# Masks of the first three units moved from VectorE to ScalarE and GpSimd, and the first two value tiles loaded from GpSimd's queue

## The chip, the cores and the metric

One core of one Trainium2 chip. The metric is the device time of one execution in microseconds (us); smaller is better. "Before" and "after" are the kernel without and with the change. A kernel is called faster or slower when the interval of its ratio lies beyond 2%.

## The reference

Gated linear attention (4 batches x 8 heads, 768 steps, 48 wide), then a low-rank mixer and an MLP on the result (4 x 768 x 384):

```python
f = 1.0 / (1.0 + np.exp(-f_logit))
for t in range(S):
    state = f[:, :, t, :, None] * state + np.einsum('bhd,bhe->bhde', k[:, :, t], v[:, :, t])
    y[:, :, t] = np.einsum('bhd,bhde->bhe', q[:, :, t], state)
x = y.transpose(0, 2, 1, 3).reshape(B, S, H * D)
xt = x.transpose(0, 2, 1)
u = x + (xt @ U @ V).transpose(0, 2, 1)
return u + np.maximum(u @ w_ch1, 0.0) @ w_ch2
```

## The kernel before

Attention runs in 16 units, each two heads of a batch; `HP` is 4 units per batch. Units 0 to 3 stand alone at the start: there is no MLP work yet to put beside them. Within a unit the sequence is cut into 12 chunks of 64. The parts that matter:

```python
def load(n, *names):                       # f, k, q, v of unit n, all from SyncE's queue
    ...
    nc.sync.dma_start(out=dst[:, :, par, 0:D], in_=head.rearrange("(c p) d -> p c d", p=P))
    ...
load(0, "f", "k", "q")
load(1, "f")
load(0, "v")
load(1, "k", "q", "v")
# ... constants, then eight small GpSimd memsets, then the weight loads are defined

def scores():                              # in attend(n)
    T["A"] = two.tile([P, 2, NBL, C], F32, name="A")
    sc = ps_big.tile([P, 2, 512], F32, name="sc", tag="big")
    # 48 products k^T q into sc (PSUM)
    with tc.high_priority(offset=AHEAD):
        nc.vector.tensor_tensor(T["A"], sc[...], causal..., ALU.mult)     # the mask

def inner():                               # later: 48 products of A with v
    ...

# the first batch, in a fixed order on TensorE, VectorE and ScalarE
busy(1)                                    # dummy products, to keep TensorE going
for piece in front(0, "gates"):
    piece()
for n in range(HP):
    pieces = front(n, "keep", "keys") + rear(n - 1, "scan", "scores")
    pieces += [lambda: busy(3)] + rear(n, "kept") + front(n, "read_back", "queries")
    if n + 1 < HP:
        pieces += front(n + 1, "gates") + rear(n - 1, "read", "inner") + rear(n, "states")
    for piece in pieces:
        piece()
    if n < 2:
        load(n + 2, "v")
    if n == 1:
        for start, _ in weights[: early + 2]:      # the first of these loads U
            start()
    elif n > 1:
        load(n + 2, "f", "k", "q", "v")
```

`gates` turns f on TensorE (six transposes) and takes the sigmoid; once f of unit n is read, f of unit n + 2 is loaded into its place. **One thing matters later**: in this stretch only TensorE, VectorE and ScalarE run in the order written.

## Time and profile before

| | before |
|---|---|
| time, median of the first 3 runs (range) | 488.54 us (488.51 to 489.53) |
| span of the profiled run | 486.9 us |
| TensorE busy | 469.2 us, 96% |
| masks on VectorE | 16 |

Beside the lines that the prediction shows, two more of the page are needed. The first is the clock granted to TensorE in 40 equal slices of the span, in tenths of full speed; the second is the group of VectorE's scans called Y below.

```profile
PEclk9999999999999999999999999999999999999999
L712 DVE TENSOR_TENSOR_SCAN late<-fz,other 128x768 f32<-128x768 f32 x16 | 27.9, 1745 | 0.1
```

Every slice has a 9 (90% or more). The row says less than it seems to: the trace's first clock record, of full speed, begins at 10.99 us, and a stretch without a record is drawn as full speed. Before that TensorE was slower, as the prediction's lines show: six transposes take 1.51 us at 6.60 and 0.85 us at 20.02, the filler 3.43 us and later 2.13. From 10.99 to 485 us the clock did not fall in this run. The scans take 1745 ns each.

### The profile page before, as it was taken

What the parts mean: (1) busy time and instruction counts of PE and PEld (TensorE: products, weight loads), DVE (VectorE), ACT (ScalarE), POOL (GpSimd) and SP (SyncE); (2) the same over time, 40 slices, a digit from 0 to 9 for tenths busy, and PEclk for the clock granted to TensorE, in tenths of its full rate; (3) what the DMA queues carried; (4) which work ended last, traced back from release to release, by engine and by line L of the source; (5) the groups of instructions that cost most, each with busy time, mean ns of one, the idle gap of its engine ahead of it and who ended that gap; (6) DMA issues with size and microseconds to landing.
All of it is one profiled execution on the core that took longest, in us unless ns stands there. A gap on an engine that the chain in (4) does not pass through costs nothing.

```text
span 486.9 us, 12734 instructions
## 1 busy us (share of the span) xinstructions
PE 469.2 (96%) x5541; PEld 400.0 (82%) x5541; DVE 355.4 (73%) x563; ACT 163.2 (34%) x309; POOL 37.6 (8%) x49
## 2 busy tenths in 40 slices
PE   7996899999999999999999999999999999999995
PEld 4775688886566568899898888899979999999995
DVE  5887689777999857656857548797896886958642
ACT  2444666664334313423231403433231312112200
POOL 3002245453000000000000000000000000000000
PEclk9999999999999999999999999999999999999999
DMA  9979975756778512333535100100000000000001
GB/s 146 158 153 178 254 194 135 162 143 79 110 116 121 96 41 36 52 48 67 76 55 94 25 18 18 27 3 20 19 1 1 33 2 18 16 1 34 1 33 38
DMA packets 158679, 34.34 MB, mean 71 GB/s; under 512 B 149206, under 2 KB 157078, under 8 KB 158614
## 3 DMA queue, kind: packets, MB, share of 16 engines
q1 hardware_dynamic: 158614, 33.44, 37.0%
q8 instruction: 45, 0.74, 0.6%
q14 instruction: 20, 0.16, 0.1%
HBM read 28.70 MB, written 4.72 MB: 69 GB/s over the span
## 4 chain that ended last, share of the span: by engine, by line
PE 79%; DVE 10%; DMA 3%; issue 3%; ACT 2%; SPq 2%; DVEq 0%; ACTq 0%
PE pw L312 26%; PE pz L258 23%; PE pp L410 11%; PE y L863 2%; PE pt L660 2%; PE sc L788 2%; PE ds L825 2%; PE y L881 2%; PE po L283 2%; PE idle L962 2%; PE put L246 1%; DMA late<-in_f_logit_dram 1%; DVE late L694 1%; DVE late L712 1%; PE pt L809 1%
## 5 line engine op out<-in xcount | busy, mean ns | idle before, releaser
L258 PE MATMUL pz<-uT,w 128*128 128x256 f32 x504 | 115.7, 383 | 0.3 <-ACT uT L247 0.3
L258 PEld LDWEIGHTS pz<-uT,w 128*128 128x128 f32 x504 | 93.4, 190 | 13.3 <-issue 0.5
L312 PE MATMUL pw<-w,z_all 128*128 128x192 f32 x216 | 37.7, 329 | 0.0
L312 PE MATMUL pw<-zw,w_raw 128*128 128x192 f32 x216 | 37.4, 327 | 0.0
L312 PEld LDWEIGHTS pw<-zw,w_raw 128*128 128x128 f32 x216 | 35.2, 190 | 0.8 <-issue 0.6
L312 PEld LDWEIGHTS pw<-w,z_all 128*128 128x128 f32 x216 | 35.0, 190 | 0.7
L95 POOL TENSOR_TENSOR w<-w_y,w_r 128x384 int32<-128x384 int32 x24 | 31.5, 1311 | 41.5 <-DVE w_y L94 36.5
L694 DVE TENSOR_TENSOR_SCAN late<-fz,late 128x768 f32<-128x768 f32 x16 | 28.1, 1755 | 8.9 <-ACT fz L689 4.2
L268 ACT ACTIVATE z_all<-pz 128x512 f32<-128x512 f32 x33 | 19.7, 596 | 41.4 <-PE pz L258 41.3
L410 PE MATMUL pp<-v_nat,late 128*128 128x128 f32 x224 | 28.8, 275 | 0.0
L712 DVE TENSOR_TENSOR_SCAN late<-fz,other 128x768 f32<-128x768 f32 x16 | 27.9, 1745 | 0.1
L410 PEld LDWEIGHTS pp<-v_nat,late 128*128 128x128 f32 x224 | 27.0, 192 | 0.0
L283 PE MATMUL po<-w,zw 128*128 128x384 f32 x72 | 25.6, 499 | 0.0
L283 PE MATMUL po<-w,z_all 128*128 128x384 f32 x72 | 25.3, 496 | 0.3 <-DVE o L187 0.3
L403 ACT ACTIVATE other<-other 128x512 f32<-128x512 f32 x18 | 11.3, 631 | 39.9 <-DVE other L187 39.9
L851 ACT COPY st<-added 128x576 f32<-128x576 f32 x12 | 14.7, 1224 | 27.5 <-DVE added L846 27.5
L92 DVE TENSOR_SCALAR w_y<-w_y 128x384 f32<-128x384 f32 (+3 forms) x27 | 13.1, 485 | 14.0 <-ACT w_y L90 13.8
L795 DVE TENSOR_TENSOR A<-sc,causal 128x768 f32<-128x768 f32 x16 | 15.2, 947 | 10.7 <-PE sc L788 10.7
L283 PEld LDWEIGHTS po<-w,z_all 128*128 128x128 f32 x72 | 13.1, 190 | 8.7 <-DVE o L187 0.9
L283 PEld LDWEIGHTS po<-w,zw 128*128 128x128 f32 x72 | 12.9, 189 | 8.7 <-issue 1.2
L187 DVE TENSOR_TENSOR w_raw<-z_all 128x768 f32<-128x768 f32 x12 | 11.4, 954 | 10.6 <-ACT z_all L268 9.2
L312 PE MATMUL pw<-w,other 128*128 128x192 f32 x108 | 18.6, 327 | 0.0
(193 smaller groups left out, 825.6 us busy)
## 6 DMA issues: line engine op xcount, KB each, us to landing
w_raw<-in_moe_w_ch_dram SPq DMA_DIRECT2D x18, 384.0 KB, 3.9
out_dram<-o SPq DMA_DIRECT2D x24, 192.0 KB, 1.9
v_nat<-in_v_dram SPq DMA_DIRECT2D x16, 144.0 KB, 3.6
v_nat<-in_v_dram SPq DMA_DIRECT2D x32, 72.0 KB, 3.3
zw<-in_moe_w_ch_dram SPq DMA_DIRECT2D x6, 384.0 KB, 5.7
late<-in_f_logit_dram SPq DMA_DIRECT2D x10, 96.0 KB, 3.1
late<-in_k_dram SPq DMA_DIRECT2D x10, 96.0 KB, 3.0
late<-in_q_dram SPq DMA_DIRECT2D x10, 96.0 KB, 2.6
```

The costliest lines, as they stand in the source:

```text
L92: nc.vector.tensor_scalar(f, f, SMALLEST, LARGEST, ALU.max, ALU.min)
L95: nc.gpsimd.tensor_tensor(dst.bitcast(I32), shaped(y.bitcast(I32)), shaped(r), ALU.add)
L187: nc.vector.tensor_tensor(*args)
L258: nc.tensor.matmul(pm[:, i * 2 * P : (i + 1) * 2 * P], lhsT=w1[:, m, o : o + P], rhs=uT[a][:, m, :], start=(m == 0), stop=(m == NDC - 1))
L268: nc.scalar.activation(z[a, c][:, k : k + 2, :].rearrange("p i t -> p (i t)"), pm, AF.Relu)
L283: nc.tensor.matmul(pm, lhsT=z[a, i // NI][:, i % NI, s * P : (s + 1) * P], rhs=w2[:, i, :], start=(i == 0), stop=(i == NFC - 1))
L312: nc.tensor.matmul(pm[:, n * HM : (n + 1) * HM], lhsT=lhs[:, i, :], rhs=rhs[:, i, :], start=(i == 0), stop=(i == NI - 1))
L410: nc.tensor.matmul(pm[:, i, r * P : (r + 1) * P], lhsT=room["w"](wn)[:, r * P : (r + 1) * P], rhs=x_node(a, xn), start=((xn, wn) == of[0]) ...
L694: nc.vector.tensor_tensor_scan(backwards(X, S - 1, S), backwards(f, S, S), backwards(ends, S - 1, S), 0.0, ALU.mult, ALU.add,)
L712: nc.vector.tensor_tensor_scan(Y, f[:, 0:S], starts, 0.0, ALU.mult, ALU.add)
L795: nc.vector.tensor_tensor(T["A"], sc[:, :, 0 : NBL * C].rearrange("p h (c i) -> p h c i", i=C), causal.unsqueeze(1).unsqueeze(1).broadcast ...
L851: nc.scalar.copy(st, states.rearrange(by_e, c=NCH))
```

## The change

Its intent is to free VectorE, which looks full in the first units, of three masks, and SyncE of six transfers. The masks of units 0 to 2 become a ScalarE copy from PSUM to SBUF and two GpSimd selects in place. The v loads of units 0 and 1 go to GpSimd's queue, behind its memsets.

```diff
+            queue = nc.gpsimd if nm == "v" and n < 2 else nc.sync
...
-                        nc.sync.dma_start(
+                        queue.dma_start(
...
-                    nc.sync.dma_start(out=dst[:, :, par, 0:D], ...)
+                    queue.dma_start(out=dst[:, :, par, 0:D], ...)
...
     load(1, "f")
-    load(0, "v")
-    load(1, "k", "q", "v")
+    load(1, "k", "q")
...
         nc.gpsimd.memset(wholes[i][:, 0:1], 0.0)
+    load(0, "v")
+    load(1, "v")
...
+            if n < HP - 1:
+                nc.scalar.copy(T["A"].rearrange("p h c i -> p h (c i)"), sc[:, :, 0 : NBL * C])
+                for s in part:
+                    half = T["A"][s].rearrange("p h c i -> p (h c) i")
+                    nc.gpsimd.affine_select(out=half, in_=half, compare_op=ALU.is_ge, fill=0.0, base=0,
+                                            pattern=[[0, 2 * NBL], [1, C]], channel_multiplier=-1)
+                return
             with tc.high_priority(offset=AHEAD):
                 nc.vector.tensor_tensor(
```

## The prediction

> **What bounds the kernel now.** I read the page first, then the chain that ended last in order of time, then the instructions in order of time for the first 58 us, because both halves of the change act only on units 0 to 2 and their loads, which lie in that stretch. Last I read each load's issue and landing there and the windows table.
>
> ```profile
> PE 469.2 (96%) x5541; PEld 400.0 (82%) x5541; DVE 355.4 (73%) x563; ACT 163.2 (34%) x309; POOL 37.6 (8%) x49
> PE 79%; DVE 10%; DMA 3%; issue 3%; ACT 2%; SPq 2%; DVEq 0%; ACTq 0%
> L795 DVE TENSOR_TENSOR A<-sc,causal 128x768 f32<-128x768 f32 x16 | 15.2, 947 | 10.7 <-PE sc L788 10.7
> ```
>
> TensorE is the bound: busy for 96% of the span, 79% of the chain. The masks that the change moves are L795, 947 ns each on VectorE, 16 in all; the change moves three.
>
> Now the chain through the first units (columns: start, duration, what):
>
> ```profile
> 6.60 1.51 PE pt L660 x6
> 8.12 3.43 PE idle L962 x6
> ...
> 14.68 5.21 DMA late<-in_f_logit_dram
> 20.02 0.85 PE pt L660 x6
> ...
> 25.72 2.13 PE idle L962 x6
> 27.85 0.52 PE pt L809 x12
> 28.38 1.46 PE pt L660 x12
> ```
>
> The reader is to see that the chain here is TensorE from 6.60 us on, with one break, a transfer of f for unit 2 that ends at 20.02. "PE idle L962" is filler: three dummy products that the program puts on TensorE in each round while VectorE makes the keys. The change does not take them away, so TensorE cannot pass them earlier. How much VectorE has to spare behind them is in the timeline:
>
> ```profile
> 18.76 0.93 DVE L795 TENSOR_TENSOR A<-sc,causal 128x768 f32<-128x768 f32 x1
> 19.99 0.64 PEld L660 LDWEIGHTS pt<-ident,late 128*128 128x128 f32 x6 [0.74 <-DVE A L795]
> 20.02 0.85 PE L660 MATMUL pt<-ident,late 128*128 128x128 f32 x6 [0.53 <-DMA late<-in_f_logit_dram]
> 22.29 0.92 PE L881 MATMUL y<-v_nat,A 64*64 64x48 f32 x48 [0.26 <-ACT seen L870]
> 24.75 0.96 DVE L672 TENSOR_TENSOR kz<-pt,late 128x768 f32<-128x768 f32 x1 [0.17 <-PE pt L660]
> 25.65 2.20 PE L962 MATMUL idle<-late,ident 128*128 128x384 f32 x6
> 27.79 0.59 PE L809 MATMUL pt<-ident,kz 64*128 64x64 f32 x12
> ```
>
> Unit 2's keys (kz) are done at 24.75 + 0.96 = 25.71, but the transposes that read them (L809) start at 27.79, when the filler ends: 2.1 us to spare. Mask 0 is done at 19.69 and its reader (L881) starts at 22.29: 2.6 us to spare. VectorE looks full here (2.76 to 3.00 busy of each 3 us between 18 and 30), yet its work is not what TensorE waits for. The one place where the mask shows is 20.02: the transposes of f for unit 2 take over the PSUM buffer of scores 0, free only when the mask has read it, and they also wait for the load of f. Both end within 0.3 us of each other, and the wait is 0.53 us.
>
> The transfers (columns from the left: window, its length, PE, PEld, DVE, ACT, POOL busy, clock, DMA share, GB/s):
>
> ```profile
> 6.00:9.00 3.00, 2.61 (x10) 2.01 (x9) 1.81 (x2) 0.93 (x3) 0.00 (x0) 1.00 1.51 164
> 12.00:15.00 3.00, 3.00 (x69) 2.71 (x66) 1.49 (x2) 2.23 (x4) 0.00 (x0) 1.00 1.50 169
> 15.00:18.00 3.00, 3.00 (x56) 1.85 (x54) 2.93 (x6) 0.29 (x2) 0.00 (x0) 1.00 1.42 171
> ```
>
> The DMA engines are full and move 164 to 171 GB/s, whatever is asked. A unit's tile of f, k, q or v is two heads of 144 KB; 288 KB at 167 GB/s is about 1.8 us. The landings agree: f of unit 1 lands at 10.0, v of unit 0 at 12.0, k of unit 1 at 13.6, q at 15.1, v of unit 1 at 17.3 and f of unit 2 at 19.9 us, one tile per 1.9 us or so (issue plus its time to landing). SyncE's queue runs some 5 us ahead of the landings, so it waits for the engines, not they for it.
>
> **What the Trainium skill says.** "DMA: Bandwidth & Descriptors", section "Issuing engines are not separate DMA queues": transfers from SyncE, ScalarE and GpSimd run on the same 16 engines, and a second issuer saves only issue time. The constant 164 to 171 GB/s at over 90% busy agrees that issue is not the limit. The same page, "Queues, rings and completion order": each engine goes round-robin between queues that have work; with one queue, the trace before cannot show it. "Latency and other measured facts" there: first byte about 1 us from GpSimd's software path against 0.6 us; no instance in this trace. "SBUF — State Buffer", section "Who interferes with whom": a VectorE instruction with two SBUF inputs and a GpSimd instruction that reads SBUF exclude each other. VectorE's scans (L694, L712, L846) have two, and GpSimd is idle from 5.4 to 42.3 us, so the trace before shows neither side of it.
>
> **The change part by part.** First, it takes three masks from VectorE: 3 x 0.93 = 2.8 us of VectorE work. On the path this counts only where TensorE waits for it: at 20.02, at most 0.53 us.
>
> Second, it adds three ScalarE copies of 128x768 from PSUM. The copy of the same size at L815 takes 0.80 us. Copy 0 would follow the small copy at 16.26 to 16.47 and run to 17.3, when ScalarE is idle before (2.47 us idle until 18.94); copies 1 and 2 lie in such gaps too (2.23 us each). Cost on the path: 0.
>
> Third, it adds six GpSimd selects of 64x768. The trace has selects of 64x64 at 0.235 us and 128x128 at 0.286, so my estimate is 0.235 + 704 x (0.051 / 64) = 0.80 us, 1.6 us for a pair; a fill of 768 elements took 0.74. Mask 0 would be ready at 17.3 + 1.6 + 0.2 for hand-over = 19.1; with two scans excluding it (1.35 and 1.75) up to 22.2, just before its reader at 22.29. Masks 1 and 2 have more room. A held scan costs VectorE at most 2 x 0.8 us per unit, against 0.93 saved and 2.1 us to spare. One tighter thread: a held scan of states (17.50) holds ScalarE's copies L813 and L815 and with them the products L863 at 20.80; slack 0.5 us, loss up to 0.3. Sum: 0 to +0.3.
>
> Fourth, the six v transfers go from SyncE to GpSimd. SyncE saves 2.5 us (6.25 to 8.80) and 2.4 us (11.59 to 13.96) of issue; f of unit 2 is issued near 9 rather than 14.09. But the engines have the same bytes to move before it, unless v goes slower than now. If v takes half of every engine from 6.5 us on, v of both units is through after 4 x 1.9 = 7.6 us, at 14.1, well ahead of its readers for unit 1 (22.98). Meanwhile q of unit 0 and f of unit 1 get half the rate: f lands near 13 (needed at 12.71, now 10.0) and k of unit 1 near 15.5 (needed 14.30, now 13.6), a delay of some 1.2 us, from which the vanished 0.53 wait is taken back: net +0.7. If v takes a third or less, f and k are in time and f of unit 2 is early: net -0.5. v of unit 0 has 13.46 - 12.0 = 1.5 us to spare.
>
> Sum: -0.5 from the wait at 20.02, 0 to +0.7 from the order of loads, 0 to +0.3 from held scans. I take -0.5 + 0.3 = -0.2, to one decimal, and put the time at 488.3. From 56 to 110 us TensorE is busy for all of 54.00 us, so a shift of the start goes through whole, neither grown nor lost.
>
> **The rivals.** (1) VectorE is the bound in the first units, as its busy share suggests; then three masks give 2.8 us: 485.7. For it: 2.90 of 3 us busy. Against: 2.1 us of slack behind the filler, and the chain. (2) GpSimd's path for v is slow: 768 pieces of 192 bytes per head made by software. v of unit 0 then lands after 13.46 and all of TensorE shifts; if a transfer takes 2.5 us to issue, the third is out at 5.4 + 7.5 = 13, landing at 15: +1.5, so 490. Nothing in this trace rules that out. (3) A second queue keeps the engines fuller, and loads come faster than 170 GB/s; then the 0.53 vanishes and no load is late: 488.0. (4) The gaps called "issue" at 40.42 (1.72 us) and 44.92 (1.94), each following a 16 KB packet of the instruction queue, change with the load on the engines: 1 us either way.
>
> **Range and chances.** Best -1.5 (0.5, and 1 from rival 4), worst +1.5 (rival 2 or late k); I widen slightly for the spread of the runs before (488.51 to 489.53): 486.9 to 489.9. Two per cent is 9.8 us, more than three times the whole of what any part could move, so: within 2% 0.97, faster 0.02, slower 0.01.
>
> **What would show it.** Right: L795 x13; VectorE idle longer before kz or waiting for transposes; filler and L809 back to back still; the 0.53 wait at 20.02 gone or replaced by one for k or f of unit 1 near 13 to 15 us; TensorE's first large product (L258, 55.84) within 1 us of before. Wrong: L258's start earlier by 2 us or more (rival 1), a TensorE wait for v_nat near 13.5 (rival 2), or an end that moves while 55.84 does not.

## More of the kernel before

The order of SyncE's and GpSimd's instructions is chosen by the scheduler at build time.

Line numbers shift: before's L660, L712, L795, L809, L825 and L881 are L663, L715, L806, L820, L836 and L892 after.

## The result, and the profile after

After took **495.39 us** (median of 4 runs, 492.7 to 495.52), before 488.52 (median of 4, 487.26 to 489.53). The ratio is 1.0129, 95% interval 1.0087 to 1.017: the same within 2%, yet outside the predicted range of 486.9 to 489.9. Ratios here are the mean time of one kernel's fast runs over that of the other's of the same rounds, so not quite the ratio of the medians quoted. Executions over 1.5% slower than the fastest of the same kernel are left out of the means.

The lines of after's page that answer to those of before:

```profile
PE 474.1 (96%) x5541; PEld 404.3 (82%) x5541; DVE 355.0 (72%) x560; ACT 165.9 (34%) x312; POOL 52.8 (11%) x61
PEclk9988799999999999999999999999999999999998
PE 74%; DVE 13%; DMA 5%; issue 3%; ACT 2%; SPq 2%; POOL 1%; DVEq 0%; POOLq 0%; ACTq 0%
L715 DVE TENSOR_TENSOR_SCAN late<-fz,other 128x768 f32<-128x768 f32 x16 | 29.2, 1824 | 0.1
L806 DVE TENSOR_TENSOR A<-sc,causal 128x768 f32<-128x768 f32 x13 | 12.4, 952 | 10.9 <-PE sc L791 10.9
```

Three masks have left VectorE (L806 x13). TensorE is busy for 4.9 us more with the same 5541 products, so products took longer, and the clock's row says where: slices 3 to 5, from 25 to 62 us, are no longer 9. The transfers' share of the chain went from 3% to 5%.

To see where the time went I matched TensorE's products one to one between the two traces:

| TensorE's start of | before | after | later by |
|---|---|---|---|
| transposes of keys, unit 0 | 11.47 | 10.48 | -0.99 |
| transposes of f, unit 2 | 20.02 | 21.26 | 1.24 |
| products with mask 0 | 22.29 | 23.80 | 1.51 |
| transposes of keys, unit 2 | 27.79 | 31.47 | 3.68 |
| product 680 of 5541 | 39.22 | 43.05 | 3.83 |
| first large product (L258) | 55.84 | 61.72 | 5.88 |
| last product | | | 5.90 |

The first row is the chance of the start: the first record of full clock begins at 8.60 us in after, at 10.99 in before, and between 6.21 and 11.45 us in the twenty traces (9.02, 9.20 and 10.43 in three traces of one program). Everything is decided by 62 us; from there on the shift stays at 5.87 to 5.90. It grows in two steps, after 22 us and between 43 and 62 us. TensorE in order of time in the first of them (start, duration, what, and in brackets the idle time before it and what ended that):

```profile
13.18 0.89 PE L836 MATMUL ds<-v_nat,kb 64*64 64x48 f32 x42 [0.40 <-DMA v_nat<-in_v_dram]
...
21.26 0.85 PE L663 MATMUL pt<-ident,late 128*128 128x128 f32 x6 [2.06 <-DMA late<-in_f_logit_dram]
...
23.80 1.53 PE L892 MATMUL y<-v_nat,A 64*64 64x48 f32 x48 [0.35 <-ACT seen L881]
25.08 1.53 PE L836 MATMUL ds<-v_nat,kb 64*64 64x48 f32 x48
```

v of unit 0 comes 0.40 us late (it landed at 13.13 instead of 12.03, and TensorE was 1 us early). f of unit 2 comes 2.06 us late, against 0.53 before: it landed at 21.12 instead of 19.89, and TensorE was ready for it 0.30 us earlier. No wait for a mask appears: the products with mask 0 (L892) wait 0.35 us for a small copy as before (0.26). But they take 1.53 us instead of 0.92. The windows show why (columns as in the prediction's windows; the clock is the number after the five engines, and the DMA share behind it adds up packets that overlap, so that it can exceed 1). Before:

```profile
24.00:27.00 3.00, 3.00 (x58) 2.25 (x58) 2.76 (x7) 0.75 (x2) 0.00 (x0) 1.00 0.53 102
51.00:54.00 3.00, 2.16 (x24) 1.21 (x20) 2.48 (x4) 0.24 (x1) 0.43 (x1) 1.00 0.96 270
```

After:

```profile
21.00:24.00 3.00, 2.39 (x58) 2.12 (x62) 1.24 (x2) 1.03 (x3) 0.00 (x0) 0.71 0.96 178
24.00:27.00 3.00, 3.00 (x98) 2.91 (x95) 1.16 (x4) 0.92 (x2) 0.00 (x0) 0.50 1.18 160
27.00:30.00 3.00, 3.00 (x56) 2.42 (x55) 1.88 (x2) 0.99 (x3) 0.00 (x0) 0.65 0.77 143
...
51.00:54.00 3.00, 3.00 (x60) 1.70 (x52) 2.38 (x7) 2.43 (x7) 0.97 (x2) 0.50 1.01 218
```

TensorE ran **at half its clock** from 22.3 to 29.1 us and again from 46.2 to 56.4 us (from the trace's clock records). The first stretch lies right behind the long wait for f and brings the shift from 1.2 to 3.7. The second begins behind the first of two gaps called "issue" and holds the other (1.53 us ending at 45.78, 1.09 at 50.34; before has the same two gaps, 1.72 and 1.94). These are 1.04 us shorter in after, and still the shift grows by 2.05 there; so that stretch cost about 3.1 us. Both stretches together make about 5.5 of the 6.

The Trainium skill describes this clock in "TensorE: Matmul & The Clock Gate", "Part 1: The HAM clock gate": half speed by default and after an idle window, full speed after a busy one, windows of 4096 cycles at 1.2 GHz (3413 ns) that run freely and are not set by the kernel. The traces agree on the size: stretches at half clock last 3.4, 6.8 or 10.2 us, and begin at another phase in each run.

Why is f late? SyncE's own queue in after (issues, same columns):

```profile
8.24 3.01 SPq L550 DMA_DIRECT2D other<-in_q_dram  x2
11.29 1.45 SPq L81 DMA_DIRECT2D w_raw<-in_moe_U_dram  x1
12.86 3.43 SPq L550 DMA_DIRECT2D late<-in_f_logit_dram  x2
```

The scheduler, with six loads fewer on SyncE, has put **U's load ahead of f of unit 2**. U is 192 KB (as the trace's list of DMA issues has it) and not needed until much later; in before it stood behind v of unit 3. f of unit 2 was issued at 12.86, only 1.2 us earlier than before (14.09), and landed 1.23 us later.

### The profile page after: what moved, and what is told of

It is laid out like the page before. It is cut to its first block, busy times and chain, and to the rows that moved or that the text cites.

```text
span 493.3 us, 12757 instructions
## 1 busy us (share of the span) xinstructions
PE 474.1 (96%) x5541; PEld 404.3 (82%) x5541; DVE 355.0 (72%) x560; ACT 165.9 (34%) x312; POOL 52.8 (11%) x61
## 4 chain that ended last, share of the span: by engine, by line
PE 74%; DVE 13%; DMA 5%; issue 3%; ACT 2%; SPq 2%; POOL 1%; DVEq 0%; POOLq 0%; ACTq 0%
PE pw L312 25%; PE pz L258 19%; PE pp L410 11%; PE y L892 2%; PE y L874 2%; PE sc L791 2%; DMA late<-in_f_logit_dram 2%; PE ds L836 2%; DVE late L715 2%; DMA v_nat<-in_v_dram 2%; PE po L283 2%; DVE late L697 2%; PE put L246 1%; PE pt L663 1%; DVE added L857 1%
## 5 line engine op out<-in xcount | busy, mean ns | idle before, releaser
L258 PE MATMUL pz<-uT,w 128*128 128x256 f32 x504 | 115.7, 383 | 0.3 <-ACT uT L247 0.3
L258 PEld LDWEIGHTS pz<-uT,w 128*128 128x128 f32 x504 | 93.4, 190 | 13.3 <-issue 0.5
L697 DVE TENSOR_TENSOR_SCAN late<-fz,late 128x768 f32<-128x768 f32 x16 | 28.1, 1756 | 10.9 <-ACT fz L684 6.2
L715 DVE TENSOR_TENSOR_SCAN late<-fz,other 128x768 f32<-128x768 f32 x16 | 29.2, 1824 | 0.1
L892 PEld LDWEIGHTS y<-v_nat,A 64*64 64x64 f32 x768 | 14.8, 150 | 7.2 <-issue 3.8
L806 DVE TENSOR_TENSOR A<-sc,causal 128x768 f32<-128x768 f32 x13 | 12.4, 952 | 10.9 <-PE sc L791 10.9
L874 PEld LDWEIGHTS y<-st,qT 48*64 48x64 f32 x704 | 14.3, 145 | 6.0 <-issue 5.5
```

The source lines that it names most:

```text
L258: nc.tensor.matmul(pm[:, i * 2 * P : (i + 1) * 2 * P], lhsT=w1[:, m, o : o + P], rhs=uT[a][:, m, :], start=(m == 0), stop=(m == NDC - 1))
L697: nc.vector.tensor_tensor_scan(backwards(X, S - 1, S), backwards(f, S, S), backwards(ends, S - 1, S), 0.0, ALU.mult, ALU.add,)
L715: nc.vector.tensor_tensor_scan(Y, f[:, 0:S], starts, 0.0, ALU.mult, ALU.add)
L874: nc.tensor.matmul(o(c % 2, par, c // 2), lhsT=T["q"][rows[par], chunk[c]], rhs=T["st"][rows[par], c, :], start=(c <= 2), stop=False, skip ...
L892: nc.tensor.matmul(o(s, par, c), lhsT=T["A"][part[s ^ par], par, c, :], rhs=vt[part[s ^ par], c, par, :], start=False, stop=True, skip_gro ...
```

## The experiments

The theory after these views: the loads half hurts through SyncE's order, which delays f of unit 2; the wait leads to a stretch at half clock that multiplies it. The rivals: GpSimd's queue itself is slow, or splits the engines badly; the selects and copies disturb VectorE or TensorE; the gaps called "issue" grow, for example because instruction fetches are held up by loads. Where an expectation gives a letter, A is the order of SyncE's loads, D is harm from the added work, F is held-up instruction fetches. "The wait for f" is always TensorE's wait at the transposes of f of unit 2, "the second gap" the "issue" gap near 44 us, and "shift" the delay of TensorE's last product against before, all in the profiled run.

### Each half alone, and the order of SyncE held

`e_masks` is before with the masks half of the diff; `e_loads` is after without it. `e_after_sp` and `e_loads_sp` are after and `e_loads` with SyncE held to the written order in the first batch's loop (U then stands behind f of unit 2):

```diff
-        for n in range(HP):
-            pieces = ...
+        with tc.manual_schedule(engines={nc.sync.engine}):
+            for n in range(HP):
+                pieces = ...                      # the loop's body, indented
```

> Masks of units 0 to 2 by ScalarE and GpSimd; value tiles still from SyncE's queue (its order is then that of before). Theory A (the loss is made by the loads: SyncE's order of loads changes, f of unit 2 lands late, TensorE waits 2 us and its clock is halved afterwards): within 1 us of before, 487.5 to 489.5, granted clock 0.995 or more, no stretch at 0.5 clock. Theory B (the loss is made by the masks: GpSimd's selects take 2.1 us each and hold VectorE's scans): slower by 3 to 7 us, 491.5 to 495.5.

> Value tiles of units 0 and 1 from GpSimd's queue; masks as before on VectorE. SyncE's order comes out as in the changed kernel, with the load of U ahead of f of unit 2. Theory A: as the changed kernel, 492.5 to 496, a TensorE wait of about 2 us on f of unit 2 and a stretch of about 7 us at half clock after it. Theory B: 487.5 to 489.5, no such wait.

> The changed kernel with SyncE's loads held in the order of the program for the first four units (so that U stays behind the loads of unit 3, as before; the rest of its order is unchanged but for one weight tile). Theory A1 (the order of SyncE's queue is the cause): f of unit 2 lands before TensorE needs it, no half clock, 487 to 489.5. Theory A2 (GpSimd's queue itself is the cause: its transfers are late or take the others' share): the wait on v of unit 0 near 13 us stays at 0.4 us or more, and a wait on f, k or q of units 1 or 2 of 1 us or more stays: 491 to 495.

> As the run before (order of SyncE's loads held), but masks on VectorE. Both theories: within 1 us of that run if the masks do nothing; a difference of over 1.5 us between the two would mean that the masks matter once the loads are in order (theory B in part).

Measured, before at 488.51 (7 runs, 487.9 to 489.92):

| kernel | us, median of 4 | ratio, 95% | wait for f | at half clock, first 60 us | shift |
|---|---|---|---|---|---|
| e_masks | 491.20 | 1.0048 (1.0024 to 1.0072) | 1.33 | 22.7-26.1, 50.0-53.4 | 2.84 |
| e_loads | 490.69 | 1.0060 (0.9998 to 1.0122) | 2.31 | 23.3-26.7 | 2.40 |
| e_after_sp | 490.95 | 1.0034 (1.0004 to 1.0065) | 0.48 | 48.5-51.9, 55.3-58.7 | 2.26 |
| e_loads_sp | 488.45 | 0.9992 (0.9968 to 1.0016) | 1.42 | 46.8-50.2 | -0.16 |

`e_loads_sp` has the loads on GpSimd's queue and takes before's time: **the queue itself costs nothing**. With the order left to the scheduler the same loads cost 2.2 us by the medians (three runs of `e_loads` took 489.8 to 491.4, one 495.36, so its interval reaches 1), and on after, holding the order gains 4.4 us. TensorE is ready for f at the same time in `e_loads` and `e_loads_sp` (18.89 and 18.95); f landed at 21.06 and 20.24. **By their times the first three expectations missed**: each lies between the ranges of its two theories, in keeping with a cost in both halves. In `e_after_sp` f of unit 2 is issued at 10.73, 3.4 us earlier than before, yet:

```profile
19.91 0.84 PE L663 MATMUL pt<-ident,late 128*128 128x128 f32 x6 [0.48 <-DMA late<-in_f_logit_dram]
```

TensorE reads it at 19.91, against 20.02: the same bytes lie ahead of it on the DMA engines, as the prediction had argued. By the medians the masks half costs some 2.5 us, with the loads half (`e_after_sp` over `e_loads_sp`) and without it (`e_masks` over before).

### U's load moved ahead in before, and the wait filled in after

`e_uhoist` does to before's SyncE the first thing that the scheduler did, and no more:

```diff
+        weights[0][0]()                           # U's load, ahead of f of unit 2
         busy(1)
...
-                for start, _ in weights[: early + 2]:
+                for start, _ in weights[1 : early + 2]:
```

> The kernel before with one load moved: U's weights are issued by SyncE ahead of f of unit 2 instead of behind unit 3; nothing from GpSimd, masks as before. If the order of the loads is what the loads' half cost (theory A1): f of unit 2 lands near 21 us instead of 19.9, TensorE waits 1.5 us or more there, time 489 to 494 (1.2 us for the landing, the rest if the clock is halved after the wait). If GpSimd's queue had to take part (A2): within 0.7 us of before.

Measured: 492.48 us (median of 4; 488.37 to 493.11), ratio 1.0052 (1.0004 to 1.0100), before 488.51. The wait for f grew to 1.77 us, half clock at 22.6-26.0 and 49.9-53.3, shift 4.49. The three runs at 492 to 493 had a mean clock of 0.988 to 0.992, and the one at 0.999 took 488.37. So U ahead of f, with no other part of the change, can cost 4 us, when the clock falls. But this run shows the order less purely than it was meant to. f landed at 20.36, 0.47 us later than in before and not near 21 as expected. The rest of the longer wait comes from TensorE, which was ready for f at 18.73 instead of 19.49: its full clock began at 8.92 us, not at 10.99.

`e_after_fill` is after with dummy products where TensorE waits for f, so that it is late but not idle:

```diff
+                pieces += ([lambda: busy(5)] if n == 1 else [])
                 pieces += front(n + 1, "gates") + rear(n - 1, "read", "inner") + rear(n, "states")
```

> The changed kernel with five more dummy products on TensorE ahead of the transposes of f of unit 2, where it waited 2.06 us; the wait stays, but TensorE is busy in it. If the half clock after the wait is what costs (theory C): no stretch at 0.5 clock between 21 and 30 us, L881-like products of unit 0 at 0.92 us again, 1.5 to 2.5 us faster than the changed kernel: 491.5 to 494. If the half clock has another cause or costs nothing: 495 to 496.

Measured: 495.69 us (495.02 to 496.84), ratio 1.0142 (1.0113 to 1.0170). **The time missed the expectation**, for two reasons. Five dummy products (two instructions each) took 3.39 us, more than the wait of 2.06 that they were to fill, and so f's transposes began at 22.29, 1.0 us later than in after. And the later gaps (1.64 near 37, 1.80, 2.23 us) brought half clock at 39.6-43.0 and 53.3-56.7. But the point it was built for came out. The windows where after ran at 0.71, 0.50 and 0.65:

```profile
21.00:24.00 3.00, 3.00 (x53) 2.25 (x53) 0.29 (x2) 0.85 (x2) 0.00 (x0) 1.00 0.90 173
24.00:27.00 3.00, 2.65 (x118) 2.26 (x108) 2.16 (x4) 1.46 (x5) 0.00 (x0) 1.00 1.28 155
27.00:30.00 3.00, 2.94 (x55) 2.01 (x54) 2.91 (x3) 1.56 (x3) 0.80 (x1) 1.00 0.76 141
```

Full clock throughout. The keys of unit 2 were transposed at 30.35, 1.1 us earlier than in after, though f's transposes had begun 1.0 us later. It was the idle time that brought the first stretch at half clock, not the late data as such.

How long a wait does that take? Over all twenty profiled runs (before and after among them), sorted by the wait for f:

| wait for f | runs | of these with half clock right after it (from 22 to 24 us) |
|---|---|---|
| none to 1.08 us | 10 | 0 |
| 1.12 to 1.42 us | 7 | 3 |
| 1.77 to 2.31 us | 3 | 3 |

Between 1.1 and 1.4 us it is a matter of the run, in keeping with windows that run freely. So is the wait itself. In all seven runs of the middle row the full clock had begun before 10 us, and TensorE was early; in before, `e_after_sp`, `e_nosel` and `e_early_f` it began after 10.9 us, and the waits are 0.26 to 0.53 us. A wait of this size is thus no sign of what the edit did.

### What in the masks half costs?

`e_dummy` is before with the copies and selects added on a spare tile, VectorE's masks kept. `e_nosel` copies the scores on ScalarE and masks nothing: its result is wrong.

```diff
+            if n < HP - 1:                        # e_dummy
+                nc.scalar.copy(spare_A, sc[:, :, 0 : NBL * C])
+                for s in part:
+                    half = spare_A[s]...
+                    nc.gpsimd.affine_select(out=half, in_=half, ...)
+            if n < HP - 1:                        # e_nosel
+                nc.scalar.copy(T["A"]..., sc[:, :, 0 : NBL * C])
+                return
```

> The kernel before with all that the masks' half adds and nothing that it removes: ScalarE copies scores 0 to 2 to a spare tile and GpSimd selects there, while VectorE still makes the masks that are used. If the added work does harm by holding VectorE or ScalarE (theory D): 490.5 to 492 as with the masks moved. If the harm comes from the masks being late or from what VectorE's new timing does (theory E): 487.5 to 489.5.

> The kernel before with the masks of units 0 to 2 replaced by ScalarE's copies alone, without GpSimd's selects; the result is wrong on purpose (no mask in those units). Theory D: 487.5 to 489, the harm is gone with the selects. Theory E (taking VectorE's masks away is itself what changes the waits of TensorE and its clock): 490.5 to 492 as with selects.

Measured: `e_dummy` 488.94 us, 0.9997 (0.9964 to 1.0030); `e_nosel` 488.87, 1.0020 (0.9987 to 1.0053). Added work alone shows no cost, and **taking three masks off VectorE gains nothing**, which is what the slack behind the filler said. Neither half of the masks' move shows a cost by itself.

`e_early_f` is before with v of unit 1 behind f of unit 2 on SyncE, to take the wait for f away. `e_early_f_masks` adds the masks half, `e_early_f_b2` takes one dummy product of three out of the filler, and `e_masks_again` is `e_masks` once more.

```diff
-    load(1, "k", "q", "v")
+    load(1, "k", "q")
...
         for piece in front(0, "gates"):
             piece()
+        load(1, "v")
...
-            pieces += [lambda: busy(3)] + ...
+            pieces += [lambda: busy(2)] + ...     # e_early_f_b2 only
```

> The kernel before with one swap in SyncE's order: f of unit 2 ahead of v of unit 1 (which is needed only at 23 us). f should land 1.9 us earlier, near 18 us; TensorE's wait of 0.5 to 1.4 us on it goes, and with it the half clock that follows it in some executions. If that wait and its half clock are worth anything: 0.5 to 1.5 us faster, 486.5 to 488, and a narrower spread than before's 487.2 to 492. If only the gaps for instructions after 36 us matter: within 0.5 us of before.

> As the run before, with the masks of units 0 to 2 by ScalarE and GpSimd. If the masks cost through the wait on f and the half clock after it (theory E): 0 to 0.7 us from the run before. If they cost in another way, 1.5 to 3 us slower than it.

> As the first run of this call, with two dummy products in each round instead of three. If TensorE's queue with its filler is what sets the pace in units 1 to 3: up to 2.2 us faster (0.73 a round). If VectorE sets the pace once the filler is shorter: 0.5 to 1.5 us. If the filler is what keeps the clock up: slower, with stretches at half clock between 20 and 40 us.

> The masks' half alone once more, the same program as the first run of this study, for a second profile and a narrower interval. If its 2.5 us are the masks' own: 490.5 to 491.7 again, with the half clock again in the same two places. If they were the chance of that chip's executions: 487.5 to 490, and the half clock elsewhere or nowhere.

Measured in 5 rounds, before at 488.47 (11 runs; one at 957.22 is an outlier):

| kernel | us, median of 6 | ratio, 95% | wait for f | second gap | at half clock, 39 to 60 us | shift |
|---|---|---|---|---|---|---|
| e_early_f | 487.78 | 0.9967 (0.9929 to 1.0006) | 0.26 | 1.40 | 3.4 us | -0.24 |
| e_early_f_masks | 489.63 | 1.0014 (0.9978 to 1.0051) | none | 2.27 | 10.2 us | 2.85 |
| e_early_f_b2 | 487.55 | 0.9976 (0.9940 to 1.0013) | 0.62 | none | 3.4 us | -1.65 |
| e_masks_again | 490.07 | 1.0022 (0.9984 to 1.0060) | 1.12 | 2.04 | 6.8 us | 1.33 |

(`e_early_f_b2` has eight products fewer, which its shift allows for.) An early f gains 0.7 us by the medians, and one dummy product less in each round 0.2 us more; neither is clear of noise, and the second is less than the 0.5 us of its middle expectation. `e_masks_again` lies between its two, with its half clock in another place. With f early, TensorE waits for mask 0 instead, as the prediction had said of this place (in `e_early_f`; 0.62 us in `e_early_f_b2`):

```profile
20.00 0.87 PE L660 MATMUL pt<-ident,late 128*128 128x128 f32 x6 [0.26 <-DVE A L795]
```

With the masks moved as well this wait is gone. Still, with no wait there at all, the masks cost 1.9 us by the medians (489.63 against 487.78; neither ratio to before is clear of 1), and the cost sits behind 43 us: at product 680 `e_early_f_masks` is still 0.17 us ahead of before, at 1000 it is 2.84 behind. So the masks do not act through the wait for f.

### A quieter stretch around the gaps

The "issue" gaps stand 126 to 127 products apart, or about 254 instructions of TensorE, counting a weight load for each product. In before, 16 KB packets of the instruction queue move just ahead of both gaps near 40 and 45 us. That suggests instruction fetches, held up by the loads of units 4 and 5. The four `e_quiet` kernels move those loads behind the mixer's first part, with SyncE in written order throughout: before (`e_quiet`), the masks half, after, and `e_early_f`.

```diff
-            elif n > 1:
-                load(n + 2, "f", "k", "q", "v")
...
         mix_of(rest)
+        for n in (HP, HP + 1):
+            load(n, "f", "k", "q", "v")
```

> The kernel before with the loads of units 4 and 5 issued after the first units' mixing instead of beside units 2 and 3 (they are first used after 64 us), SyncE in the order of the program. Theory F: the gaps of 1.7 and 1.9 us near 40 and 45 us shrink to under 0.7 us each, no half clock before 60 us, 484.5 to 487. Theory G: the gaps stay, 487.5 to 489.5.

> As the run before, with the masks of units 0 to 2 by ScalarE and GpSimd. Theory F: within 0.7 us of the run before, the masks' 1.5 to 2.5 us are gone with the gaps. If the masks cost by themselves: 1.5 to 2.5 us slower than it.

> The whole changed kernel with the same two repairs (loads of units 4 and 5 later, SyncE in the order of the program, so U is no longer ahead of f of unit 2). Theory F and A1 together: within 1 us of the first run of this call, 484.5 to 488. If one of them is wrong: 490 or more.

> The first run of this call with f of unit 2 ahead of v of unit 1 as well; the candidate to beat both kernels: 484 to 486.5, no wait over 0.5 us on a load before 40 us.

**All four missed**: 498.28 (ratio 1.0210), 500.21 (1.0235), 499.31 (1.0216) and 496.62 us (1.0164), before at 488.59; all four intervals reach below 1.02. Units 4 and 5 now got their data too late: the shift jumps by 5.9 to 7.1 us between 66 and 82 us, with TensorE at half clock there. Nor was the stretch quiet, for the written order puts weight loads of 384 KB there; the first gap grew to 2.9 us in `e_quiet`. What can be read is the shift ahead of the jump: 1.20 for `e_quiet`, 3.75 with the masks, 3.75 for the whole change. Again the masks cost 2.5 us and the loads nothing, in one trace of each.

The kept traces show more of the gaps than these runs. I looked at four places in each of the twenty, the products near 470, 597, 723 and 850, where a gap can stand. With the waits for semaphores counted, 253 to 257 of TensorE's instructions are recorded from one place to the next (in before, after and `e_masks_third`). All 42 gaps over 0.4 us end 1.2 to 1.6 us after a 16 KB packet of the instruction queue has ended (in before: 40.54 to 42.13 and 45.51 to 46.86), and TensorE passes none of the 80 places earlier than 1.2 us after one. So **the gaps are waits for the next block of instructions**, as far as traces show it. In before the block from product 724 to 851 holds only 2.79 us of work, while the packet for the next starts 1.99 us after the block began and takes 1.38 us. Whether loads hold the packets up stays open.

### One GpSimd instruction in place of two, and the masks half a third time

`e_mult` masks with one GpSimd multiply:

```diff
-                for s in part:
-                    half = ...
-                    nc.gpsimd.affine_select(out=half, ...)
+                nc.gpsimd.tensor_tensor(T["A"], T["A"], causal..., ALU.mult)
```

> The three masks as in the masks half alone (ScalarE copies the scores, GpSimd masks them in place), but by one GpSimd multiply of 128x768 with the triangle in place of two selects of 64x768; loads as before. Three things are open on the 1.1 to 2.7 us that moved masks cost: (a) that inner() then waits for two GpSimd instructions, with a few more wait instructions in TensorE's stream, so that its gaps fall two products earlier (722 and 849 in place of 724 and 851) and the second is longer; (b) GpSimd's selects as such, or the masks coming from GpSimd at all; (c) the phase of the clock's windows, chance from build to build. If (a): gaps back at 724 and 851, the second about as in the kernel before, time 488.0 to 488.9. If (b): as the masks half alone, 489.6 to 491.3, with a second gap of 2.0 us or more. If (c): anything between, and e_masks_third of the same rounds not clearly different from the kernel before. One multiply should take about 2.6 us (a GpSimd operation of 128x384 takes 1.31 us in the page), against 3.3 to 4.2 for a pair of selects.

> The masks half alone once more, beside e_mult on one chip. The two runs so far gave 1.0048 and 1.0022 of the kernel before. If the cost of the masks is real: 1.002 to 1.006, 489.6 to 491.3 us, gaps at 722 and 849 with the second at 2.0 us or more. If it was the phase of the clock's windows by chance: an interval that holds 1.000 well inside, time below 489.

Measured in 5 rounds, before at 489.41 (11 runs, 487.18 to 492.64): `e_mult` 490.93 us (487.74 to 495.09, the last not in the ratio), ratio 1.0014 (0.9964 to 1.0065); `e_masks_third` 492.77 (488.15 to 493.98), 1.0063 (1.0022 to 1.0104). The gaps of `e_mult` stayed at products 722 and 849, the second 2.28 us: not moved back by fewer instructions, so theory (a) of its expectation falls. Its time decides nothing between the other two.

The profiled run of `e_masks_third` is the telling one, because by chance it never fell to half clock between its start and 484 us. These are its windows around the second gap:

```profile
42.00:45.00 3.00, 1.45 (x72) 1.25 (x64) 2.01 (x6) 0.64 (x1) 1.05 (x2) 1.00 1.06 165
45.00:48.00 3.00, 2.28 (x62) 1.43 (x63) 1.45 (x5) 1.94 (x7) 0.45 (x1) 1.00 1.15 180
48.00:51.00 3.00, 2.17 (x26) 1.13 (x26) 2.78 (x6) 1.94 (x5) 1.26 (x2) 1.00 1.17 203
```

It has the wait for f (0.85) and the second gap (2.27 us from 43.45 on, across the first two lines), yet the clock stays at 1.00, and it took 488.15 us, its last product 0.47 us **ahead** of before's. The same program with 6.8 us at half clock took 490.28 and 491.68 us. So the masks half need not cost anything; where the traces show its cost, it is paid as half clock. Two things limit this. Another run of `e_masks_third` took 492.29 us at a mean clock of 0.998, and has no trace to say where the time went. And why moved masks bring half clock more often is open. Between 39 and 60 us the six profiled runs with masks on GpSimd and f not delayed by U (`e_masks` three times, `e_after_sp`, `e_early_f_masks`, `e_mult`) spent 0 to 10.2 us at half clock, 6.3 on average, five with masks on VectorE or none (before, `e_loads_sp`, `e_nosel`, `e_early_f`, `e_early_f_b2`) 2.7. The six have a second gap of 2.00 to 2.28 us, the five 0 to 1.94. But `e_dummy`, whose masks stay on VectorE, had 6.8 us in its profiled run too. For the longer gap the traces give a part of a reason: where the clock was full, the block ahead of it holds 2.46 to 2.48 us of work with the masks moved (`e_nosel`: 2.47) and 2.78 to 2.82 without, so that TensorE is through it 0.3 us sooner.

## Why the prediction was wrong, point by point

- **"VectorE looks full [...] yet its work is not what TensorE waits for"**: right. Rival 1 (485.7 us) falls with `e_nosel` at 1.0020. That mask 0 and f end close together at 20.02 was right too (`e_early_f`).
- **Copies**: right, 0.80 us each in idle time of ScalarE, nothing on the path.
- **Selects, 0.80 us each, mask 0 ready between 19.1 and 22.2 as scans exclude them**: right. The pair ran from 16.68 to 20.85, ready ahead of its reader. GpSimd and VectorE in after at that time:

```profile
16.68 4.17 POOL L802 TENSOR_SCALAR_AFFINE_SELECT A<-A 64x768 f32<-64x768 f32 x2 [6.84 <-ACT A L799]
```

```profile
16.50 1.35 DVE L857 TENSOR_TENSOR_SCAN st<-added,whole 128x576 f32<-128x576 f32 x1
17.77 2.38 DVE L715 TENSOR_TENSOR_SCAN late<-fz,other 128x768 f32<-128x768 f32 x1
```

  A pair lasts 4.17 us because the instructions take turns: the first select waits for the scan that ends at 17.85; the scan L715 waits for that select and takes 2.38 us instead of 1.75; the second select waits until the scan ends at 20.15 and ends at 20.85. From the last step a select is 0.70 us by itself, my estimate from these rows. This agrees with "SBUF — State Buffer", "Who interferes with whom", which the prediction cites. In `e_mult` the multiply held the same scan to 3.31 us.
- **v from GpSimd's queue**: "a delay of some 1.2 us" for f and k of unit 1 did not come; v of unit 0 cost 0.40 us (rival 2 had 1.5). That 164 to 171 GB/s come "whatever is asked" holds for these loads only; before moves 270 GB/s from 51 to 54 us. With the order held, the queue is free of cost (`e_loads_sp`, 0.9992).
- **"f of unit 2 is issued near 9 rather than 14.09. But the engines have the same bytes to move before it"**: the step that failed first. It took SyncE's remaining order as given. The build put U's 192 KB ahead of f, which was issued at 12.86 and landed 1.23 us later. So the term of -0.5 for the wait at 20.02 became +1.53. With the order held the sentence is true (f landed at 19.77 and 20.24, against 19.89). Shown by `e_after_sp`, by `e_loads` beside `e_loads_sp`, and in part by `e_uhoist`.
- **"so a shift of the start goes through whole, neither grown nor lost", and a sum made of waits alone**: the step that failed in size. Behind 62 us it holds (5.87 to 5.90). Ahead of that the sum lacks a term for TensorE's clock: a wait grown by 1.5 us brought 6.8 us at half clock, and the shift went from 1.2 to 3.7; 10.2 us more lie around the gaps near 45 and 50 us, some 3.1 us of time. I gave the term nothing, and it measured about 5.5 us. The clock row before was all 9, and I took it as a fixed property, though the skill's page on the clock was at hand and TensorE had gaps of 1.7 and 1.9 us already. The prediction's own lines held the sign: the same six transposes take 1.51 us at 6.60 and 0.85 at 20.02. So the times at which it has TensorE need a load (12.71, 13.46) rest on where the slow start ended, and in after they came about 1 us earlier.
- **Rival 4, "1 us either way"**: the gaps themselves changed within that (after's are 1.03 us shorter). What follows them was not in it.
- **The range**: its worst case, +1.5 on 488.54, is 490.04, and rival 2 has 490; both lie above the stated 489.9. The measured time lies far outside either way.
- **The check "L258 within 1 us of before"** was the right one to look at: 5.88 us says at once that the loss lies in the first 62 us.

The share of each half in after's 6.9 us: about 4.4 through SyncE's order (after to `e_after_sp`; without the masks it is 2.2, `e_loads` to `e_loads_sp`), about 2.5 with the masks (`e_after_sp` to `e_loads_sp`), and nothing for the queue. The first is explained: order, wait, clock. The second is measured several times (ratios 1.0048, 1.0022 and 1.0063) and its last step seen (half clock), but what starts it is not.

No version clearly beats before: the best, `e_early_f` and `e_early_f_b2`, gain 0.2 to 0.3% with intervals that reach 1.

## What to carry to other kernels

Moving loads to another queue also rewrites the order of those that stay, if a scheduler orders that queue: compare both queues' issue order before you count what moved, and pin it if the order matters. A wait of TensorE of more than about 1 us may cost a multiple of its length, because the clock can fall to half for 3.4 us or more after it; look at the clock row, check its first microseconds by comparing the same instruction early and late, and judge such kernels by several runs, as the same program differs by up to 6 us (before: 486.92 to 493.06). An engine that looks full but has slack behind a filler gives nothing when relieved.

## What the Trainium skill lacked or had wrong

- "TensorE: Matmul & The Clock Gate" ("HAM oscillation — how this bites in real kernels") gives the rule that TensorE shouldn't idle for more than about 3.4 us. Here half clock followed waits of 1.1 to 1.4 us in 3 of 7 runs and of 1.8 to 2.3 us in 3 of 3; none did up to 1.08 us. Idle time of a third of a window can be enough. (The page also tells of short idle times that make the clock swing, without a length for them.)
- The same page, Part 1, puts the ramp at under 1% of a typical kernel's span. In this kernel single stretches of 6.8 and 10.2 us in the middle cost about 2.4 and 3.1 us, 1.1% of the span and more than everything the change was meant to move.
- "DMA: Bandwidth & Descriptors" ("Issuing engines are not separate DMA queues") is right that a second issuer brings no bandwidth (0.9992), but doesn't say that moving an issue can reorder what the first queue keeps, if a scheduler orders it: 4.4 us here.
- No page gives the time of a GpSimd select: 64x768 took about 0.70 us by itself, and a pair 2.8 to 4.3 us where VectorE's scans took turns with it.
- "Runtime: NRT & Kernel Launch" ("Instruction fetch mechanics") has instructions fetched in blocks of 16 KiB, 256 instructions, and calls the cost of crossing a boundary mostly hidden. The block agrees with the traces (253 to 257 recorded instructions); the cost doesn't: at 42 of the 80 crossings looked at, TensorE sat idle for 0.4 to 2.9 us.
